# Ten weight chunks of the second layer converted during batch 0's attention, with other buffers for its values and for the first weight quarter

## The chip, the cores and the metric

The kernel runs on one core of a Trainium2 chip. The metric is the device time of one execution in microseconds, as the median of the runs. TensorE (PE) multiplies matrices, VectorE (DVE), ScalarE (ACT) and GpSimd (POOL) work element by element, and SyncE (SP) issues most of the transfers. Each engine, and each queue of transfer issues, works through its instructions in the order in which they stand.

## The reference, cut to what matters

```python
scale = 1.0 / np.sqrt(q.shape[-1])

def sm_attn(qq, kk, vv):
    s = scale * np.matmul(qq, kk.transpose(0, 1, 3, 2))
    s = s - np.max(s, axis=-1, keepdims=True)
    a = np.exp(s)
    a = a / (np.sum(a, axis=-1, keepdims=True) + 1e-09)
    return np.matmul(a, vv)
p_packed = sm_attn(p, k, v)                 # batch 8, heads 8, 32 packed rows, width 64
out = sm_attn(q, p_packed, p_packed)        # 576 rows per batch and head
x = out.transpose(0, 2, 1, 3).reshape(4608, 512)
h = x @ moe_w_in                            # 512 x 2048, float64 in memory
x = (h * np.cos(h)) @ moe_w_out             # 2048 x 512, float64 in memory
h = x @ moe2_w_in
sp = np.where(h > 20.0, h, np.log1p(np.exp(np.minimum(h, 20.0))))
out = (h * np.tanh(sp)) @ moe2_w_out
```

## The kernel before

The weights stand in memory as 64-bit numbers. A chunk of 128 rows and 512 columns of one weight is 512 KB. The helper `conv` loads a chunk and makes 32-bit numbers of it: on ACT an `activation` that reads the high words (L519), on DVE a shift of the low words (L521) and a shift-and-or that joins the two (L525). A chunk of `moe_w_out`, the second layer of the first MLP (`wo1_unit`), is then split into a high and a low part for the matmuls: ACT copies the high part (L534), POOL subtracts to get the low part (L539). Its load goes into one of two buffers named `raw`, and the pieces on the way stand in `tmp` buffers. There are sixteen such chunks. The sixteen chunks of `moe_w_in` (`w_load`, four quarters of four) are converted by the same lines and multiplied by the packed attention values of a batch (L576), and ACT and DVE split the product (L592, L593) into the layer's weights `W1`. So `W1` folds the packed values of a batch into the first layer.

The first MLP runs over 16 tiles of 288 tokens, two tiles per batch, and each tile has 16 steps. A step makes one block of the hidden layer (`l1`, six matmuls into `ps`, L147 to L149), takes it through a chain on ACT, DVE and POOL that makes h cos h (L884, L886, L887, L893, L894, L901, L904), and three steps later multiplies it by one chunk of the second layer (`l2`, twelve matmuls into four `acc` banks). After the sixteenth step the tile is copied out (`evac`, L925 and L927) to `xo`.

Everything that prepares a batch stands in tables by step (`at_pe`, `at_ew`, `at_ld`), which are worked off next to the tiles' steps. Steps below 0 come before the first tile. Batch 0's attention stands at steps from -16 (`PRO`): for each of the two groups of heads g, `k_unit` transposes the keys on TensorE (`e1_pe`, `early_copy`, L201), forms the scores of the packed rows (L288), takes their maximum (L303), their exponential (L311), transposes it (L327, copied by L335 and L336), multiplies it by the values (L353), and leaves the packed result in `pk` (L379). `q_unit(0)` transposes the queries (`e0_pe`), forms the scores against `pk` (L430), and takes them through maximum, subtraction, exponential, sum and scaling (L444, L450, L451, L458, L462, L465, L466, L470) to the first operand of the first layer, `aT` (L475). `behind(mark)` holds an instruction back in the order until a marked one stands.

Within a table entry and between entries a scheduler sets the order on each engine, by priority (`hp`, `tc.high_priority`) and by its own estimate of when an operand is there. The result is one fixed order on each engine.

Before, the values of batch 0 and the first quarter of `moe_w_in` stand in the buffers of the second layer (`wo`, sixteen of them), so that no chunk of the second layer can be written there until they are used. The other three quarters of `moe_w_in` go through the four buffers named `wb`. The chunks of the second layer are placed at steps `ft + WO_OFF`, 0 to 15, their loads two steps earlier.

Of the kernel before, what the change touches and what calls it, by code (L numbers as in the profile page):

```python
# [8 lines left out]
F32 = mybir.dt.float32  # L9
# [26 lines left out]
WO_OFF = 0  # L36
Q0_T = 5
K_OFFS = ((23, 33, 38, 41), (-12, 4, 20, 36), (-4, 4, 19, 39))
# [17 lines left out]
COMB = 240  # L56
HOLD_N = 32
STOP = 0
W0E = (-1, -1, -1, -1)
# [29 lines left out]
def build(tc, q, k, v, p, w1i, w1o, w2i, w2o, out):  # L89
    nc = tc.nc  # L90
    ctx = ExitStack()
    with ctx:
# [121 lines left out]
        def k_unit(b, g, alloc_v):  # L214
# [107 lines left out]
            def s4_pe():  # L322
                e = st["e"]
                t1, t2 = ring(), ring()
                ev = e[:, :512].rearrange("p (t c) -> p c t", c=4)
                for c in range(4):
                    nc.tensor.transpose(t1[:, 128 * c : 128 * c + 128], ev[:, c], ident)  # L327
                nc.tensor.transpose(t2[:, :128], e[:, 448:576], ident)
                st["t"] = (t1, t2)
# [64 lines left out]
        def q_unit(t, pre=None):  # L394
# [25 lines left out]
            def e0_pe():  # L420
                st["kt"] = kt_tile([128, 1152])
                for h in range(4):
                    early_copy(st["kt"], early_trans(st["raw"], h, (0, 0, 1)), h, (0, 0, 1))

# [64 lines left out]

        def conv(src, shape, dst, save, wide=False, st=None, mark=None):  # L490
            st = {} if st is None else st

            def load():
                if wide == "wo":
                    r = wo_tile([128, 512, 2], I32)
                elif wide:
                    w = wab_tile(1, [128, 2048], I32)
                    r = w[:, :1024].rearrange("p (f t) -> p f t", t=2)
                    st["t"], st["m"] = w[:, 1024:1536], w[:, 1536:].bitcast(F32)
                else:  # L500
                    r = tp.tile([128, 512, 2], I32, tag="raw", bufs=2, name=nm("raw"))
                n = shape[-1] if len(shape) == 3 else 512
                if len(shape) == 3:
                    nc.sync.dma_start(r.rearrange("p (a f) t -> p a (f t)", f=n), src.bitcast(I32))
                else:
                    ins = nc.sync.dma_start(r.rearrange("p f t -> p (f t)"), src.bitcast(I32))
                    last_w[0] = getattr(ins, "ins", ins)
                st["r"] = r

            def c1():  # L510
                r = st["r"]
                if wide == "wo":
                    w = wo_tile([128, 1024], I32)
                    st["t"], st["m"] = w[:, :512], w[:, 512:].bitcast(F32)
                elif not wide:
                    st["t"] = tp.tile([128, 512], I32, tag="tmp", bufs=TMP_BUFS, name=nm("cvt"))
                    st["m"] = tmp_tile([128, 512])
                with behind(mark and ("act", *mark)):
# [27 lines left out]
        def w_load(fg, hp, fresh=False):  # L546
            st = {}
            if fresh:
# [4 lines left out]
                    lambda d: w1s.__setitem__((fg, hp), d),  # L553
                    "wo" if fg == 0 else True,
                    st,
# [43 lines left out]
        def wo1_unit(ft):  # L599
# [4 lines left out]

            return conv(w1o[128 * ft : 128 * ft + 128, :], [128, 512], dst, None)

# [171 lines left out]
        for g in range(2):  # L778
            wo = lambda sh: wo_tile(sh, F32)
            wa = lambda sh: wab_tile(0, sh, F32)  # L780
            loads, vl, stages = k_unit(0, g, wo)
            at_ld(PRO - 2, hp(loads, (4 - g) * HP_PRO))
# [17 lines left out]
        for ft in range(16):  # L800
            load, cs = wo1_unit(ft)
            n = ft + WO_OFF
            at_ld(n - 2, load)
            for i, f in enumerate(cs):
# [58 lines left out]

        for n in range(PRO - 4, 0):
            run_bg(bg_pe, n)
            run_ew(n)
# [415 lines left out]
```

## Time and profile before

| | |
|---|---|
| median of 3 runs | 1552.05 us (1551.67 to 1552.79) |
| the profiled execution | 1553.24 us, span 1551.5 us |
| mean granted TensorE clock | 0.984 |
| PE busy (matmuls) | 1472.1 us, 95% of the span |
| DVE, ACT, POOL busy | 1110.1 us (72%), 893.2 us (58%), 639.8 us (41%) |

The profiled execution's time is 1.7 us longer than its span, and 1.2 us above the median. The busy shares are means over stages with different limits; the first 120 us are read apart below. A time of an instruction or a transfer is counted from the start of the span.

### The profile page before, as it was taken

The numbers are of one execution on the slowest core, as the hardware profiler recorded it, in microseconds if no ns is written. First come the engines' busy times: TensorE is split into PE (matmuls) and PEld (weight loads), VectorE is DVE, ScalarE is ACT, GpSimd is POOL, SyncE is SP. The second block draws the span as 40 slices with busy tenths as digits, with TensorE's granted clock in tenths as the row PEclk, the third lists the DMA queues.
The fourth block names the chain that finished last, engine by engine and source line by source line (L and its number), as shares of the span: only waits on it lengthen the run. The fifth ranks groups of instructions, "written<-read, shape, count | busy, mean of one in ns | idle before, by whom it ended". The sixth has DMA issues, their size and how long they took to land.

```text
span 1551.5 us, 29143 instructions
## 1 busy us (share of the span) xinstructions
PE 1472.1 (95%) x9986; PEld 1301.5 (84%) x9986; DVE 1110.1 (72%) x2080; ACT 893.2 (58%) x1850; POOL 639.8 (41%) x634
## 2 busy tenths in 40 slices
PE   6688999999999999999999999999999999999998
PEld 4567778898987989789999887888889898888997
DVE  4895667677676877687775778678678757766756
ACT  3685767667766767667765455334443534454443
POOL 0562323245643645546754666224522512352102
PEclk9899999999999999999999999999999999999999
DMA  8889575445648546633313658668878877867886
GB/s 270 266 227 221 168 179 153 133 108 171 184 128 219 169 136 181 190 93 91 105 50 122 238 212 252 190 203 240 265 217 234 293 217 220 242 212 218 234 261 201
DMA packets 247411, 299.21 MB, mean 193 GB/s; under 512 B 103648, under 2 KB 131040, under 8 KB 247264
## 3 DMA queue, kind: packets, MB, share of 16 engines
q1 hardware_dynamic: 244976, 296.21, 64.2%
q8 instruction: 79, 1.29, 0.4%
q10 hardware_dynamic: 2288, 1.15, 0.3%
q14 instruction: 68, 0.56, 0.1%
HBM read 240.65 MB, written 56.62 MB: 192 GB/s over the span
## 4 chain that ended last, share of the span: by engine, by line
PE 45%; DVE 5%; issue 4%; DMA 3%; POOL 3%; ACT 3%; SPq 1%; DVEq 0%; POOLq 0%; ACTq 0%
PE acc L148 8%; PE acc L149 8%; PE acc L147 8%; PE ps L147 7%; PE ps L148 6%; PE ps L149 6%; POOL ws L643 1%; DMA ws<-wst 1%; DVE wab L979 1%; DVE r L887 1%; DMA raw<-in_moe_w_in_dram 1%; DVE r L886 1%; DMA wst<-ws 1%; POOL gh L1037 0%; ACT wab L978 0%
## 5 line engine op out<-in xcount | busy, mean ns | idle before, releaser
L904 POOL TENSOR_TENSOR gh<-r,gh 128x288 fp32r<-128x288 f32 x256 | 212.4, 838 | 326.1 <-ACT gh L901 227.2
L148 PE MATMUL acc<-gh,wo 128*128 128x288 f32 x1024 | 299.2, 299 | 1.0 <-POOL gh L904 1.0
L149 PE MATMUL acc<-gh,wo 128*128 128x288 f32 x1024 | 295.1, 296 | 0.0
L1037 POOL TENSOR_TENSOR gh<-t,gh 128x512 fp32r<-128x512 f32 (+1 forms) x108 | 144.0, 1337 | 353.9 <-ACT gh L1036 344.4
L147 PE MATMUL acc<-gh,wo 128*128 128x288 f32 x1024 | 276.3, 303 | 1.9 <-ACT gh L901 0.9
L148 PE MATMUL acc<-gh,T 128*128 128x512 f32 (+1 forms) x560 | 207.2, 371 | 2.4 <-DVE gh L1037 1.9
L147 PE MATMUL ps<-wab,ws 128*128 128x512 f32 (+1 forms) x560 | 206.2, 369 | 2.5 <-DMA ws<-wst 1.1
L148 PE MATMUL ps<-wab,ws 128*128 128x512 f32 (+1 forms) x560 | 206.4, 369 | 0.0
L149 PE MATMUL ps<-wab,ws 128*128 128x512 f32 (+1 forms) x560 | 205.3, 369 | 0.0
L149 PE MATMUL acc<-gh,T 128*128 128x512 f32 (+1 forms) x560 | 205.1, 369 | 0.0
L148 PEld LDWEIGHTS acc<-gh,wo 128*128 128x128 f32 x1024 | 193.4, 189 | 8.7 <-issue 5.2
L147 PE MATMUL ps<-aT,wab 128*128 128x288 f32 x512 | 162.4, 318 | 39.2 <-DVE r L894 22.2
L147 PEld LDWEIGHTS acc<-gh,wo 128*128 128x128 f32 x1024 | 183.5, 191 | 15.3 <-issue 5.3
L149 PEld LDWEIGHTS acc<-gh,wo 128*128 128x128 f32 x1024 | 192.7, 189 | 3.1 <-issue 3.0
L893 ACT ACTIVATE r<-r,halfpi 128x288 f32<-128x288 f32 x256 | 135.8, 535 | 89.3 <-DVE r L887 84.8
L1037 DVE TENSOR_TENSOR gh<-wo,gh 128x512 fp32r<-128x512 f32 (+1 forms) x160 | 129.0, 813 | 81.1 <-ACT gh L1036 80.6
L147 PE MATMUL acc<-gh,T 128*128 128x512 f32 (+1 forms) x560 | 181.9, 369 | 1.2 <-DMA T<-tst 1.1
L894 DVE TENSOR_TENSOR r<-r,ps 128x288 f32<-128x288 f32 x256 | 114.3, 449 | 74.0 <-ACT r L893 73.6
L147 PEld LDWEIGHTS ps<-aT,wab 128*128 128x128 f32 x512 | 98.9, 193 | 67.1 <-DVE r L894 30.6
L884 ACT ACTIVATE ki<-ps,quarter 128x288 int32<-128x288 f32 x256 | 125.2, 497 | 51.0 <-PE ps L149 40.8
L148 PE MATMUL ps<-aT,wab 128*128 128x288 f32 x512 | 154.3, 301 | 0.0
L149 PE MATMUL ps<-aT,wab 128*128 128x288 f32 x512 | 153.6, 300 | 0.0
(181 smaller groups left out, 3005.3 us busy)
## 6 DMA issues: line engine op xcount, KB each, us to landing
T<-tst SPq DMA_DIRECT2D x280, 256.0 KB, 3.0
ws<-wst SPq DMA_DIRECT2D x224, 256.0 KB, 3.0
ld<-ws SPq DMA_DIRECT2D x80, 256.0 KB, 3.7
kr<-in_q_dram SPq DMA_DIRECT2D x60, 272.0 KB, 5.8
kr<-in_k_dram SPq DMA_DIRECT2D x56, 272.0 KB, 5.3
tst<-wt SPq DMA_DIRECT2D x56, 256.0 KB, 2.2
wst<-ws SPq DMA_DIRECT2D x56, 256.0 KB, 2.2
x2d<-xo SPq DMA_DIRECT2D x64, 144.0 KB, 1.8
```

Source lines behind the costliest of these rows:

```text
L147: nc.tensor.matmul(ps, l0, r0, start=first, stop=False, skip_group_check=more)
L148: nc.tensor.matmul(ps, l0, r1, start=False, stop=False, skip_group_check=more)
L149: nc.tensor.matmul(ps, l1, r0, start=False, stop=last, skip_group_check=more)
L643: nc.gpsimd.tensor_tensor(w[:, 1], CB[p][K3[k]], w[:, 0], ALU.subtract)
L884: nc.scalar.activation(ki, st["h"], AF.Identity, bias=quarter, scale=1.0 / TWO_PI)
L886: nc.vector.scalar_tensor_tensor(r, ki, -TWO_PI, st["h"], ALU.mult, ALU.add)
L887: (nc.gpsimd if n % C_MOD in C_POOL else nc.vector).tensor_scalar(r, r, 1.570796, -4.712388, ALU.min, ALU.max)
L893: nc.scalar.activation(g, g, AF.Sin, bias=halfpi, scale=1.0)
L894: nc.vector.tensor_tensor(g, g, st["h"], ALU.mult)
L904: nc.gpsimd.tensor_tensor(gh[:, 1], st["g"], gh[:, 0], ALU.subtract)
L979: (nc.gpsimd if k % 2 == 0 else nc.vector).tensor_tensor(x[:, a, 1, :n], src, x[:, a, 0, :n], ALU.subtract)
L1037: eng.tensor_tensor(hl[:, 1, :n], src, hl[:, 0, :n], ALU.subtract)
```

## The change

Ten of the sixteen chunks of the second layer (`WO_EARLY`) are placed at steps -18 to -9 (`WO_AT`), their loads two steps earlier, and the first two loads get a priority ahead of, and level with, batch 0's key loads. For these ten the piece `m` stands in a `gh` buffer. The values of batch 0 go into `ld` buffers, and the first quarter of `moe_w_in` goes through the four `wb` buffers like the others. `q_unit(0)`'s transposes come one step later, and are held behind the transposes of group 1's exponential.

```diff
-Q0_T = 5
+Q0_T = 6
...
+WO_EARLY = 10
+WO_AT = tuple(-18 + ft for ft in range(10))
...
-                nc.tensor.transpose(t2[:, :128], e[:, 448:576], ident)
+                marks[("pe", 1, b, g)] = nc.tensor.transpose(t2[:, :128], e[:, 448:576], ident)
...
-                    early_copy(st["kt"], early_trans(st["raw"], h, (0, 0, 1)), h, (0, 0, 1))
+                    early_copy(st["kt"], early_trans(st["raw"], h, (1, 0, 1)), h, (1, 0, 1))
...
-        def conv(src, shape, dst, save, wide=False, st=None, mark=None):
+        def conv(src, shape, dst, save, wide=False, st=None, mark=None, alt=False):
...
-                if wide == "wo":
-                    r = wo_tile([128, 512, 2], I32)
-                elif wide:
+                if wide:
...
-                if wide == "wo":
-                    w = wo_tile([128, 1024], I32)
-                    st["t"], st["m"] = w[:, :512], w[:, 512:].bitcast(F32)
-                elif not wide:
+                if not wide:
                     st["t"] = tp.tile([128, 512], I32, tag="tmp", bufs=TMP_BUFS, name=nm("cvt"))
-                    st["m"] = tmp_tile([128, 512])
+                    if alt:
+                        st["m"] = ap.tile([128, 2, TT], F32, tag="gh", bufs=GH_BUFS, name=nm("m")).rearrange("p a t -> p (a t)")[:, :512]
+                    else:
+                        st["m"] = tmp_tile([128, 512])
...
-                    "wo" if fg == 0 else True,
+                    True,
...
-            return conv(w1o[128 * ft : 128 * ft + 128, :], [128, 512], dst, None)
+            return conv(w1o[128 * ft : 128 * ft + 128, :], [128, 512], dst, None, alt=ft < WO_EARLY)
...
-            wo = lambda sh: wo_tile(sh, F32)
...
-            loads, vl, stages = k_unit(0, g, wo)
+            loads, vl, stages = k_unit(0, g, ld_tile)
...
-            n = ft + WO_OFF
-            at_ld(n - 2, load)
+            n = WO_AT[ft] if ft < WO_EARLY else ft + WO_OFF
+            at_ld(n - 2, hp(load, (5 - 2 * ft) * HP_PRO) if ft < 2 else load)
...
-        for n in range(PRO - 4, 0):
+        for n in range(PRO - 6, 0):
```

The change moves instructions on every engine. A line of the attention stands two further down in the changed kernel (L311 is L313 there), a line of the first MLP's chain one further up (L884 is L883); the lines of `conv` and of the weight products keep their numbers. Three places are shown.

On ACT, the stretch of batch 0's attention around group 0's exponential. `sm_218` and `sm_259` hold group 0's maximum, `kt` the transposed keys, `raw` a chunk of the second layer as loaded. Before:

```order
L276 COPY pp_135<-ps_133 128x128
L201 COPY kt_137<-et_162 128x288
L276 COPY pp_172<-ps_170 128x128
L201 COPY kt_185<-et_194 128x288
L311 ACTIVATE tmp_234,sm_218<-ps_174,sm_218 128x288
L311 ACTIVATE tmp_234,sm_218<-ps_175,sm_218 128x288
L201 COPY kt_185<-et_210 128x288
```

The same stretch now:

```order
L278 COPY pp_203<-ps_201 128x128
L203 COPY kt_226<-et_235 128x288
L519 ACTIVATE m_162<-raw_119 128x512
L534 CAST wo_205<-m_162 128x512
L203 COPY kt_226<-et_251 128x288
L519 ACTIVATE m_209<-raw_152 128x512
L519 ACTIVATE m_268<-raw_166 128x512
L313 ACTIVATE tmp_285,sm_259<-ps_215,sm_259 128x288
L313 ACTIVATE tmp_285,sm_259<-ps_216,sm_259 128x288
```

The conversions of the third, fourth and fifth chunk of the second layer now stand ahead of group 0's exponential, where none stood.

On DVE, the stretch from the query scores' transposes to the transposes that end batch 0's attention. `sqs` is the softmax sum, `wab_424` and `wab_439` two chunks of `moe_w_in`'s second quarter, and `wab_417` is `W1`. Before:

```order
L444 STREAM_TRANSPOSE tmp_371<-ps_361 128x288
L525 SCALAR_TENSOR_TENSOR wab_424<-wab_424 128x512
L525 SCALAR_TENSOR_TENSOR wab_439<-wab_439 128x512
L444 STREAM_TRANSPOSE tmp_371<-ps_360 128x288
L450 TENSOR_REDUCE mx_377<-tmp_371 128x18
L593 TENSOR_TENSOR wab_417<-ps_410,wab_417 128x512
L462 TENSOR_REDUCE sqs_397<-tmp_371 128x18
L593 TENSOR_TENSOR wab_417<-ps_426,wab_417 128x512
L463 TENSOR_SCALAR sqs_397<-sqs_397 128x18
L465 RECIPROCAL rq_400<-sqs_397 128x18
L470 STREAM_TRANSPOSE tmp_415<-tmp_371 128x576
```

Now, from its beginning, with `pc_928` the packed queries `p` of batch 1 and `wab_491` and `wab_504` two chunks of the second quarter:

```order
L265 STREAM_TRANSPOSE pp_1108<-pc_928 128x128
L446 STREAM_TRANSPOSE tmp_468<-ps_458 128x288
L446 STREAM_TRANSPOSE tmp_468<-ps_457 128x288
L452 TENSOR_REDUCE mx_476<-tmp_468 128x18
L593 TENSOR_TENSOR wab_513<-ps_506,wab_513 128x512
L521 TENSOR_SCALAR wab_491<-wab_491 128x512
L464 TENSOR_REDUCE sqs_493<-tmp_468 128x18
L525 SCALAR_TENSOR_TENSOR wab_491<-wab_491 128x512
L465 TENSOR_SCALAR sqs_493<-sqs_493 128x18
L593 TENSOR_TENSOR wab_513<-ps_522,wab_513 128x512
L521 TENSOR_SCALAR wab_504<-wab_504 128x512
```

A transpose of batch 1 now stands first in this stretch, and the conversions of the second quarter, two of which were ahead of it, stand inside it.

On SP, the loads behind batch 0's queries (`in_q_dram`). Before:

```order
L179 DMA wab_122<-in_q_dram 96x4x192
L506 DMA wo_125<-in_moe_w_in_dram 128x1024
L506 DMA wo_127<-in_moe_w_in_dram 128x1024
L506 DMA wo_129<-in_moe_w_in_dram 128x1024
L506 DMA wo_131<-in_moe_w_in_dram 128x1024
L506 DMA wab_395<-in_moe_w_in_dram 128x1024
L506 DMA wab_408<-in_moe_w_in_dram 128x1024
L506 DMA wab_424<-in_moe_w_in_dram 128x1024
L506 DMA wab_439<-in_moe_w_in_dram 128x1024
L506 DMA raw_448<-in_moe_w_out_dram 128x1024
```

Now, with two chunks of the second layer (`raw_98`, `raw_100`) already issued ahead of the keys:

```order
L181 DMA wab_141<-in_q_dram 96x4x192
L506 DMA raw_119<-in_moe_w_out_dram 128x1024
L506 DMA wab_144<-in_moe_w_in_dram 128x1024
L506 DMA wab_146<-in_moe_w_in_dram 128x1024
L506 DMA wab_148<-in_moe_w_in_dram 128x1024
L506 DMA wab_150<-in_moe_w_in_dram 128x1024
L506 DMA raw_152<-in_moe_w_out_dram 128x1024
L506 DMA raw_166<-in_moe_w_out_dram 128x1024
```

And nine issues further on, where the second quarter of `moe_w_in` is loaded:

```order
L506 DMA raw_375<-in_moe_w_out_dram 128x1024
L506 DMA raw_882<-in_moe_w_out_dram 128x1024
L506 DMA raw_926<-in_moe_w_out_dram 128x1024
L235 DMA pc_928<-in_p_dram 32x4x32 x4
L506 DMA wab_491<-in_moe_w_in_dram 128x1024
L506 DMA wab_504<-in_moe_w_in_dram 128x1024
```

The second quarter's loads have moved from right behind the first quarter's to a place behind twelve chunks of the second layer and batch 1's `p`. From about the 25th step of the first MLP on, every engine's order is the same in both kernels.

## Rows read from the trace of the kernel before

**Rows 1.** Windows: busy time of each engine before and in tile 0.

```profile
core 0: us, PE busy (x) PEld busy (x) DVE busy (x) ACT busy (x) POOL busy (x), PEclk, DMA share, GB/s
0.00:42.60 42.60, 26.23 (x309) 18.25 (x309) 19.39 (x52) 16.61 (x38) 3.01 (x8) 0.93 0.75 245
42.60:117.30 74.70, 59.66 (x436) 48.05 (x436) 67.65 (x129) 58.34 (x113) 44.92 (x38) 0.88 0.89 258
```

**Rows 2.** Timeline, batch 0's attention and tile 0's end: start, duration, idle before.

```profile
16.19 0.50 ACT L311 ACTIVATE tmp<-ps,sm 128x288 f32<-128x288 f32 x1 [2.98 <-DVE sm L305]
...
31.05 0.27 ACT L379 COPY pk<-ps 128x128 f32<-128x128 f32 x1 [1.50 <-PE ps L374]
...
37.98 0.75 DVE L462 TENSOR_REDUCE sqs<-tmp 128x18 f32<-128x576 f32 x1 [1.39 <-ACT tmp L458]
...
42.59 0.61 PE L147 MATMUL ps<-aT,wab 128*128 128x288 f32 x1 [8.78 <-ACT aT L475]
...
117.29 0.69 ACT L925 COPY xo<-acc 128x288 f32<-128x288 f32 x2
```

**Rows 3.** Timeline of SP's issues: chunk loads of 512 KB.

```profile
11.86 0.43 SPq L506 DMA_DIRECT2D wo<-in_moe_w_in_dram  x1
...
16.19 0.33 SPq L506 DMA_DIRECT2D raw<-in_moe_w_out_dram  x1
...
45.08 0.33 SPq L506 DMA_DIRECT2D wab<-in_moe_w_in_dram  x1
```

**Rows 4.** DMA issues, these three alone: size, then us from issue to landing.

```profile
wo<-in_moe_w_in_dram SPq DMA_DIRECT2D x1, 512.0 KB, 7.6
...
raw<-in_moe_w_out_dram SPq DMA_DIRECT2D x1, 512.0 KB, 10.7
...
wab<-in_moe_w_in_dram SPq DMA_DIRECT2D x1, 512.0 KB, 4.0
```

**Rows 5.** Groups of ACT, 5 to 42.6 us (the last: tile 0).

```profile
L519 ACT ACTIVATE wo<-wo 128x512 f32<-128x512 f32 x4 | 2.5, 665 | 0.0
...
L201 ACT COPY kt<-et 128x288 f32<-128x288 f32 x6 | 2.3, 400 | 7.6 <-PE et L190 7.5
L311 ACT ACTIVATE tmp<-ps,sm 128x288 f32<-128x288 f32 x4 | 2.0, 500 | 3.0 <-DVE sm L305 3.0
...
L335 ACT COPY tmp<-ps 128x512 f32<-128x512 f32 x2 | 1.2, 587 | 5.9 <-PE ps L327 5.9
...
L534 ACT CAST wo<-tmp 128x512 fp32r<-128x512 f32 x16 | 9.9, 616 | 4.9 <-DVE tmp L525 4.5
```

**Rows 6.** Groups of DVE by form, 20 to 42.6 us.

```profile
L525 DVE SCALAR_TENSOR_TENSOR wo<-wo 128x512 int32<-128x512 int32 x4 | 2.7, 684 | 0.2 <-ACT wo L519 0.2
...
L521 DVE TENSOR_SCALAR wo<-wo 128x512 int32<-128x512 int32 x4 | 1.4, 421 | 0.0
```

**Rows 7.** Tile p of batches 1 on, 40 to 160 us: its transfers.

```profile
DMA to landing us min/median/max: 3.0/4.7/5.7
```

**Rows 8.** Groups of DVE by form, 42.6 to 117.3 us.

```profile
L525 DVE SCALAR_TENSOR_TENSOR tmp<-tmp,cvt 128x512 int32<-128x512 int32 x16 | 14.6, 918 | 0.4 <-ACT tmp L519 0.3
L521 DVE TENSOR_SCALAR cvt<-raw 128x512 int32<-128x512 int32 x14 | 10.4, 743 | 1.4 <-DMA raw<-in_moe_w_out_dram 1.4
```

**Rows 9.** Line L539, 0 to 140 us: min/median/max ns, first and last start.

```profile
L539 POOL TENSOR_TENSOR wo<-tmp,wo x16: 1274/1511/1749, 44.3 to 110.8; 128x512 fp32r<-128x512 f32 x16
```

**Rows 10.** Windows: tile 0 in four stretches, columns as in group 1.

```profile
42.60:50.30 7.70, 6.92 (x34) 3.86 (x34) 6.10 (x7) 4.32 (x8) 5.87 (x4) 0.71 0.91 272
50.30:60.00 9.70, 3.92 (x16) 3.86 (x16) 9.12 (x20) 8.61 (x18) 3.21 (x4) 0.69 1.02 311
60.00:100.00 40.00, 34.15 (x241) 27.41 (x240) 39.26 (x73) 30.82 (x60) 24.46 (x22) 0.91 0.78 246
100.00:117.30 17.30, 14.67 (x150) 12.92 (x148) 13.17 (x31) 14.59 (x31) 11.38 (x11) 1.00 1.06 251
```

More of the change, by code (lines that the diff above doesn't have):

```diff
@@ L422, in e0_pe @@
                 for h in range(4):
-                    early_copy(st["kt"], early_trans(st["raw"], h, (0, 0, 1)), h, (0, 0, 1))
+                    early_copy(st["kt"], early_trans(st["raw"], h, (1, 0, 1)), h, (0, 0, 1))
             def s2_pe():
```

## Prediction

> **What bounds the kernel now.** I read the busy time by stage first. TensorE is 95% busy over the whole span, so what counts is where it waits, and that is at the start: until 42.6 us it is busy 26.2 us, and in tile 0, from the first matmul of the first layer at 42.59 us to the copying out of the tile at 117.3 us, 59.7 of 74.7 us [rows 1, 2]. In that tile the busiest engine is DVE with 67.65 us; before it, DVE works only 19.4 of 42.6 us [rows 1]. The reader is to see a DVE that is half idle in batch 0's attention and nearly full in tile 0, with the sixteen chunk conversions of the second layer in the full part. The change moves ten of them into the half-idle part. It can gain what DVE's stage shortens by, and lose what batch 0's attention lengthens by, since all of tile 0 starts from that attention's last product. Three lengths decide: the time of the first layer's first matmul (the start, 42.59 now), the length of tile 0 (74.7 now), and their sum (117.3 now). Behind it the orders soon agree and nothing in them gives time back, so I take a shift of the sum as a shift of the end.
>
> **The start: when the loads land.** In the new order on ACT, the conversions of the fourth and fifth chunk stand ahead of group 0's exponential. An engine that waits for a load holds everything behind it, so the exponential can't start before the fifth chunk has landed. Behind keys, `p`, values and queries, the third load of 512 KB was issued at 11.86 us and landed 7.6 later, at 19.5; the ninth was issued at 16.19 and landed 10.7 later, at 26.9 [rows 3, 4]. That is six loads in 7.4 us, one per 1.24 us: the transfers run one behind the other. In the new order the blocks are the same size, only two stand ahead of the keys. So the third chunk is still the third block, and the fifth, which stands behind three chunks, the four loads of the first quarter and one more chunk, is the ninth. It lands at 26.9 us, and after its conversion (0.665 [rows 5]) the exponential starts at 27.6 us, where it was 16.19 [rows 2]: 11.4 later. If the two early blocks fill time in which the transfers now idle, the ninth lands up to 2.5 us (two blocks) sooner.
>
> **The start: ACT's stream.** From that exponential to group 1's `pk` ACT now has, in its order, four exponentials (0.500), nine L519 (0.665), seven L534 (0.616), two L335 (0.587), two L201 (0.400) [rows 5], and two each of L336 and L379, both taken at 0.27 [rows 2]: 2.0 + 6.0 + 4.3 + 1.2 + 0.8 + 1.1 = 15.4 us. The last two L534 follow their own L519 at once and must wait for a shift-and-or on DVE each (0.684 [rows 6]): 1.4 more, if nothing else stands between. So `pk` is there at 27.6 + 16.8 = 44.4 us, where it was 31.3 [rows 2]: 13.1 later. With the sooner landing and no wait it is 40.5.
>
> **The start: from `pk` to the first matmul.** That took 42.59 - 31.32 = 11.3 us [rows 2]. Two things are put in. DVE must first transpose batch 1's `p`, whose transfers stand on SP behind two more chunk loads that need the buffers of the ninth and tenth chunk back. These come free about when `pk` is made; the transfers then land 4.7 us later (3.0 to 5.7 [rows 7]), some 3 us after the scores are there. And the sum of the exponentials (37.98 us now, 6.7 after `pk` [rows 2]) stands behind the first chunk of the second quarter, which can be loaded only when its `wb` buffer has been used, and lands 4.0 us after its issue [rows 3, 4]; that ends at about the same time as the wait for `p`, so the two are not added. I take 2 us for both, between nothing (the waits lie beside each other and beside the chain) and 4 (`p` wholly exposed). The start is then 44.4 + 11.3 + 2.0 = 57.7 us, 15.1 later than now; the bounds are 40.5 + 11.3 = 51.8 and 60.
>
> **Tile 0.** DVE's work there falls by ten shift-and-ors and eight shifts (two were already done before it). At the means of this stage, 0.918 and 0.743 [rows 8], that is 15.1 us; at those before the stage, 0.684 and 0.421, when POOL hardly works [rows 1, 6], it is 10.2. One chunk of the second quarter (0.684 + 0.421 = 1.1) and two transposes come in, some 2.5 together as an estimate from the same rows. So DVE's work becomes 55.0 to 59.9 us; I take the middle, 57.5, as POOL keeps two thirds of its work there.
>
> The longer durations stand where POOL makes the low parts of the same chunks, sixteen times 1.5 us [rows 9]. The Trainium skill's page "SBUF — State Buffer", section "Who interferes with whom", says that a VectorE operation that uses both port pairs and a GpSimd operation lock each other out for a whole instruction. By that page the ten conversions' excess goes with POOL's ten pieces, the work becomes 55.0, and the sum below comes out 2.5 us smaller.
>
> To the work comes DVE's idle time. Now it is 1.6 + 0.6 + 0.7 + 4.1 = 7.0 us over four stretches [rows 10]. The first two, 2.2 us, grow: the third quarter's first load goes out 2.5 us after the first matmul and lands 4.0 later [rows 2, 3, 4], its conversion stands ahead of the first chain, and until then DVE has only a conversion and a split, some 1.8 us, where it had the second layer's chunks to fill the wait. 6.5 - 1.8 is 4.7, so the idle time becomes 4.7 + 0.7 + 4.1 = 9.5 us, and tile 0 takes 67.0 us, 7.7 less than now. Bounds: 59.7, TensorE's own busy time in the stage [rows 1], and 70.
>
> **The sum.** 15.1 later and 7.7 shorter: 7.4 us slower. The profiled execution had 1553.24 us, 1.2 above the median; against that one the sum is 1560.6, against the median of 1552.05 it is 1559.5. The other edits cost nothing that I can see: the `ld` buffers take the values while the `ld` loads of batch 1 are far off, the `gh` buffers are used by the chains only after the tenth chunk, and the query transposes, which leave the way of group 0's exponential, gain nothing as that waits for its load.
>
> **Rivals.** *The loads don't hold the streams, and it is faster.* If the chunks are there when ACT comes to them, five L519 and three L534 (5.2 us) stand ahead of the exponential, most of it in ACT's idle time (16.6 busy of 42.6 [rows 1]); say 2 us late. `pk` then comes at 18.2 + 16.8 = 35.0, the start at 48.3, and tile 0, with a DVE less idle at its beginning, takes 64: 112.3, or 5.0 faster, 1547. It decides from a start before 47.2 with my 67.0, or before 50.2 with 64. For it speaks that ACT has the room; against it that a load in this stretch took 7.6 to 10.7 us to land. *Tile 0 takes up the whole delay.* If TensorE runs through it without waiting, it takes 59.7, and 57.7 + 59.7 = 117.4: no change, 1552. Against it stands that DVE has 57.5 us of work in chains of three engines. *The four `wb` buffers hold the later quarters too.* One more wait of 4.7 us at the fourth quarter moves the tile's end from 57.7 + 67.0 = 124.7 to 129.4 us, 12.1 later than now: 1564. For it: all four quarters share four buffers now. Against it: in tile 0 DVE was nearly full from 60 to 100 us with three quarters of them in the same buffers [rows 10].
>
> That the change doesn't do what it says can be left out: the ten pieces stand ahead of the first matmul in every engine's order.
>
> **How the numbers follow.** My forecast, 1559.5, has 0.48, the faster rival 0.24, the one without change 0.16, the one with the later quarters 0.12. The range runs from the faster rival's 1547 to 1566, where a start of 60 with a tile of 70 would end it (130 against 117.3 is 12.7, so 1565). 0.2%, or 3.1 us, is about what a measurement of this kernel can tell from no change; faster by more than that gets 0.24, within it 0.16, slower 0.60.
>
> **What would show it.** In the changed kernel's profile group 0's exponential would start near 27.6 us with ACT waiting for `raw` ahead of it, `pk` of group 1 near 44, the first matmul of the first layer between 56 and 60, DVE idle for some 5 us after it, and the first tile's copying out near 125. The prediction is wrong if the exponential starts before 22 us, if the first matmul stands before 50, or if tile 0 takes less than 60 us.

## The result and the profile after

The changed kernel takes 1571.68 us (median of 4 runs, 1569.53 to 1573.14), the kernel before beside it 1552.42 (4 runs): a ratio of 1.0120, interval 1.0102 to 1.0138. It is 1.2% or 19.3 us slower, where 7.4 us were forecast. The profiled execution had 1572.67 us, its span 1570.1. In the diff of the change one line is not the kernel's: of `q_unit(0)`'s early work only the transposes moved to a later mark, `early_copy` keeps its mark `(0, 0, 1)`.

First the busy time by stage, as in [rows 1]: columns are the stretch, its length, busy time of PE, PEld, DVE, ACT and POOL with their counts, granted clock, DMA share, GB/s. The cut is the first matmul of the first layer; the last row is a piece of tile 0.

```profile
0.00:60.30 60.30, 29.04 (x308) 19.95 (x308) 33.32 (x70) 27.70 (x56) 17.25 (x18) 0.94 0.80 257
60.30:141.50 81.20, 64.12 (x403) 51.77 (x403) 57.10 (x114) 47.82 (x93) 27.43 (x26) 0.79 0.75 198
...
100.30:110.30 10.00, 5.07 (x22) 1.89 (x22) 9.68 (x18) 7.62 (x12) 5.30 (x5) 0.51 0.42 154
```

The start is at 60.30 us, 17.7 later than in [rows 1]. Tile 0 has 10.6 us less work on DVE and takes 81.2 us, 6.5 more than before. DVE now stands idle for 81.2 - 57.1 = 24.1 us of it (7.0 before), and TensorE's matmuls are busy 64.1 us instead of 59.7 at a granted clock of 0.79 instead of 0.88. In the piece from 100.3 it is 0.51, with DVE full.

The timeline of ACT, as in [rows 2] (start, duration, instruction, and in brackets the idle time ahead of it and who ended it), with lines 2 higher than before up to the attention's end:

```profile
25.69 0.68 ACT L519 ACTIVATE m<-raw 128x512 f32<-128x512 f32 x1 [5.39 <-DMA raw<-in_moe_w_out_dram]
26.97 0.67 ACT L519 ACTIVATE m<-raw 128x512 f32<-128x512 f32 x1 [0.59 <-DMA raw<-in_moe_w_out_dram]
27.53 0.49 ACT L313 ACTIVATE tmp<-ps,sm 128x288 f32<-128x288 f32 x1
...
45.84 0.27 ACT L381 COPY pk<-ps 128x128 f32<-128x128 f32 x1
...
99.58 0.67 ACT L519 ACTIVATE wab<-wab 128x512 f32<-128x512 f32 x1 [3.80 <-DMA wab<-in_moe_w_in_dram]
...
141.47 0.70 ACT L924 COPY xo<-acc 128x288 f32<-128x288 f32 x2
```

Group 0's exponential stands directly behind the fifth chunk, for which ACT waits until 26.97. Of the fourth quarter's last pair of chunks ACT gets the first only at 99.58, 39.3 us behind the start. SP's queue in tile 0 shows when they were issued (start, duration, what is issued, how often):

```profile
62.84 0.81 SPq L506 DMA_DIRECT2D wab<-in_moe_w_in_dram  x2
...
70.43 8.46 SPq L506 DMA_DIRECT2D wab<-in_moe_w_in_dram  x3
...
79.47 0.36 SPq L506 DMA_DIRECT2D wab<-in_moe_w_in_dram  x1
79.88 2.46 SPq L154 DMA_DIRECT2D kr<-in_q_dram  x4
...
83.03 1.02 SPq L154 DMA_DIRECT2D kr<-in_k_dram  x2
...
87.27 1.52 SPq L154 DMA_DIRECT2D kr<-in_k_dram  x2
...
90.80 0.99 SPq L506 DMA_DIRECT2D wab<-in_moe_w_in_dram  x2
```

The last pair is issued 30.5 us behind the start, after eight transfers of queries and keys, and its first chunk takes 8.8 us to its use. DVE's waits in tile 0 (who waited for whom, total us, times, longest), before:

```profile
DVE r L894 <- ACT r L893: 2.3, 3, 1.4
DVE cvt L521 <- DMA raw<-in_moe_w_out_dram: 1.4, 2, 1.2
DVE wab L521 <- DMA wab<-in_moe_w_in_dram: 0.8, 1, 0.8
```

and now:

```profile
DVE wab L521 <- DMA wab<-in_moe_w_in_dram: 6.2, 3, 2.9
DVE wab L593 <- ACT wab L592: 4.4, 2, 2.8
DVE pp L265 <- DMA kr<-in_q_dram: 3.8, 1, 3.8
DVE kt L160 <- DMA kr<-in_k_dram: 3.5, 1, 3.5
DVE r L893 <- ACT r L892: 3.2, 4, 1.2
DVE kt L160 <- DMA kr<-in_q_dram: 1.0, 1, 1.0
```

Waits for landings (`DMA`) make up 14.5 us of them, where they were 2.2 before. So 12.3 of the 17.1 us by which DVE's idle time grew are waits for loads. In stretches as long as those of [rows 10], except for the last:

```profile
60.30:68.00 7.70, 7.53 (x34) 4.55 (x34) 2.12 (x5) 1.81 (x4) 1.59 (x1) 0.61 0.51 175
68.00:77.70 9.70, 6.42 (x31) 6.14 (x35) 8.79 (x20) 8.35 (x16) 2.68 (x4) 0.65 0.49 163
77.70:117.70 40.00, 30.97 (x219) 24.40 (x212) 29.13 (x54) 22.98 (x43) 14.31 (x14) 0.87 0.68 199
117.70:141.50 23.80, 19.20 (x125) 16.68 (x123) 17.06 (x38) 14.68 (x32) 8.85 (x9) 0.78 1.06 218
```

DVE's idle time in them is 5.6, 0.9, 10.9 and 6.7 us; it was 1.6, 0.6, 0.7 and 4.1. And TensorE's timeline at its longest wait inside tile 0, the fourth quarter's products:

```profile
97.42 0.29 PE L151 MATMUL acc<-gh,wo 128*128 128x288 f32 x1
105.23 1.93 PE L576 MATMUL ps<-wab,pk 64*32 64x512 f32 x8 [7.52 <-DVE wab L525]
...
107.74 0.44 PE L151 MATMUL ps<-aT,wab 128*128 128x288 f32 x1
107.98 0.44 PE L149 MATMUL ps<-aT,wab 128*128 128x288 f32 x1
...
111.20 0.29 PE L149 MATMUL ps<-aT,wab 128*128 128x288 f32 x1
111.33 0.29 PE L150 MATMUL ps<-aT,wab 128*128 128x288 f32 x1
```

The loads explain only the first part of this wait: the first chunk of the pair is there at 99.58, and its shift-and-or (L525) starts at 103.34, as DVE's order puts five other instructions behind the chunk's shift, and ends at 105.08. Behind the wait the matmuls start 0.24 us apart, at 111.2 us 0.13: the lower of the clock's two levels (1.2 GHz), then the higher (2.4).

The delay at tile 0's end, 141.47 against 117.29, is 24.2 us. It stays between 22.7 and 24.6 through all sixteen tiles and is 23.9 at the last one's end. The spans differ by 18.6 only. The other 5.3 us are a difference in the second MLP, whose order is the same on every engine: from the sixteenth tile's end to the span's it took 712.5 us in the profile before, 707.2 in this one, and between 707.2 and 711.4 in those of the other kernels below. So it is not shown that the change gives them back.

### The profile page after: what moved, and what is told of

Read it like the earlier page. It is cut to its first block, busy times and chain, and to the rows that moved or that the text cites. A ratio compares the mean times of both kernels' runs of the same rounds, so it can differ in the third digit from the quotient of the medians.

```text
span 1570.1 us, 29139 instructions
## 1 busy us (share of the span) xinstructions
PE 1479.1 (94%) x9986; PEld 1308.4 (83%) x9986; DVE 1109.0 (71%) x2080; ACT 897.6 (57%) x1850; POOL 637.8 (41%) x634
## 4 chain that ended last, share of the span: by engine, by line
PE 51%; DVE 4%; DMA 2%; ACT 2%; issue 1%; POOL 1%; SPq 0%; DVEq 0%; ACTq 0%; POOLq 0%
PE acc L150 9%; PE acc L149 9%; PE acc L151 9%; PE ps L149 8%; PE ps L151 8%; PE ps L150 8%; DMA raw<-in_moe_w_in_dram 1%; DVE r L886 1%; DVE r L885 1%; DMA tst<-wt 0%; POOL wt L678 0%; ACT r L892 0%; DVE r L893 0%; DVE wab L978 0%; PE ps L576 0%
## 5 line engine op out<-in xcount | busy, mean ns | idle before, releaser
L150 PE MATMUL acc<-gh,wo 128*128 128x288 f32 x1024 | 302.8, 300 | 1.4 <-POOL gh L903 1.4
L151 PE MATMUL acc<-gh,wo 128*128 128x288 f32 x1024 | 302.0, 301 | 0.0
L149 PE MATMUL acc<-gh,wo 128*128 128x288 f32 x1024 | 278.3, 302 | 2.4 <-ACT gh L900 2.4
L150 PEld LDWEIGHTS acc<-gh,wo 128*128 128x128 f32 x1024 | 196.4, 192 | 8.8 <-issue 4.9
L151 PEld LDWEIGHTS acc<-gh,wo 128*128 128x128 f32 x1024 | 195.3, 191 | 3.0 <-issue 3.0
L149 PEld LDWEIGHTS acc<-gh,wo 128*128 128x128 f32 x1024 | 184.7, 191 | 15.5 <-ACT gh L900 5.0
L883 ACT ACTIVATE ki<-ps,quarter 128x288 int32<-128x288 f32 x256 | 125.4, 498 | 49.8 <-PE ps L151 39.5
```

The costliest lines, as they stand in the source:

```text
L149: nc.tensor.matmul(ps, l0, r0, start=first, stop=False, skip_group_check=more)
L150: nc.tensor.matmul(ps, l0, r1, start=False, stop=False, skip_group_check=more)
L151: nc.tensor.matmul(ps, l1, r0, start=False, stop=last, skip_group_check=more)
L883: nc.scalar.activation(ki, st["h"], AF.Identity, bias=quarter, scale=1.0 / TWO_PI)
```

## The experiments

The theory after this reading was that two causes add up: the start is late as early conversions wait for their loads in ACT's and DVE's order, and tile 0 is long as all four quarters now pass through four `wb` buffers. The rivals: the conversions' work itself, the lower clock, and DVE's work as the prediction had it. This table holds the two stages of every kernel, from the same windows as above: the start, tile 0's length, in it DVE's work, the time in which TensorE stood still (length less PE busy), and the granted clock. The last column is how much later than before the sixteenth tile ended.

Each row is one profiled execution. Its time lay between 5.5 us above (w_first) and 3.7 below (late4b) the median of its kernel, so differences of two or three us between rows are not shown to come from the edit. Nor is tile 0 always the same work: the scheduler sets a new order for every kernel, and in the kernels without added matmuls between 387 (hold) and 441 (eight_in_wo) were recorded in it. The ratios that are given with the runs are of medians.

| kernel | start | tile 0 | DVE | PE idle | clock | tile 16 |
|---|---|---|---|---|---|---|
| before | 42.6 | 74.7 | 67.7 | 15.0 | 0.88 | 0 |
| changed | 60.3 | 81.2 | 57.1 | 17.1 | 0.79 | 23.9 |
| staging_alone | 45.4 | 77.3 | 70.0 | 18.4 | 0.89 | 3.3 |
| eight_in_wb | 57.6 | 75.8 | 56.0 | 14.6 | 0.83 | 13.4 |
| eight_in_wo | 59.2 | 79.6 | 56.2 | 15.1 | 0.83 | 19.1 |
| no_loads | 52.1 | 78.7 | 55.7 | 16.0 | 0.81 | 15.8 |
| less_dve | 43.5 | 70.4 | 54.3 | 11.2 | 0.89 | -2.2 |
| w_first | 61.4 | 83.8 | 56.2 | 19.9 | 0.84 | 35.2 |
| hold | 58.3 | 73.9 | 56.9 | 16.7 | 0.91 | 20.1 |
| hold_w_first | 56.0 | 82.2 | 60.5 | 19.9 | 0.84 | 19.0 |
| fourth_in_wo8 | 62.5 | 66.8 | 54.6 | 9.1 | 0.91 | 13.7 |
| before_fourth | 43.5 | 77.9 | 70.7 | 15.4 | 0.85 | 2.9 |
| less_dve_fourth | 44.6 | 72.0 | 56.1 | 10.1 | 0.86 | 1.1 |
| late4b | 41.2 | 75.3 | 69.5 | 15.0 | 0.90 | -2.8 |
| filled | 61.5 | 83.7 | 55.1 | 18.5 | 0.90 | 32.3 |
| before_filled | 43.6 | 82.9 | 68.9 | 19.9 | 0.86 | 10.0 |
| late4b_filled | 43.7 | 76.8 | 67.1 | 16.7 | 0.87 | 1.2 |

**Parts of the change: staging alone, eight chunks, the first quarter back in `wo`.**

```
-WO_EARLY = 10
+WO_EARLY = 0    # staging_alone
+WO_EARLY = 8    # eight_in_wb, eight_in_wo
...
-                    True,
+                    "wo" if fg == 0 else True,    # eight_in_wo
```

> No second-layer chunk is converted early; the values stay in ld and the first quarter in wb as in the changed kernel. Theory (two causes: early conversions wait for their loads and hold ACT and DVE, so the start is late; and all four quarters share four wb buffers, so tile 0 is longer): the start falls back to 43 to 47 us, but tile 0 stays at 80 us or more, since the loads of the third and fourth quarter still wait for their buffers; time 1560 to 1567. Rival (what costs is the early conversions' work on ACT and DVE, and the lower clock behind it): both go back, start 43 to 45, tile 0 at 75, time 1551 to 1554.

> Eight early chunks instead of ten, first quarter in wb as in the changed kernel; the control for the next kernel. Theory: the third to fifth chunk still stand ahead of group 0's exponential, so the start is 56 to 60 us, tile 0 79 to 83, time 1567 to 1571. Rival (each early chunk's work costs the same): two chunks of ten less, one fifth of the 19 us back, 1567 to 1568, with the gain at the start.

> Eight early chunks, the first quarter staged in eight of the sixteen wo buffers again. Theory: the start stays late, 55 to 60 us, but the second and third quarter have their wb buffers sooner and tile 0 falls to 66 to 71, so the time is 8 to 14 below that of eight chunks with the quarter in wb: 1554 to 1562. Rival (tile 0 is long through the clock, or through the loads of batch 1's keys and of tile 1's queries): tile 0 stays at 78 or more, time within 3 us of the control.

Measured: staging alone 1.0027 (1.0012 to 1.0042), start 45.4, tile 0 77.3. So the start rises by 2.8 and the tile by 2.6 with no conversion moved; the 80 us that the theory wanted for tile 0 are not there. But this is not the staging by itself. The later query transposes stay in, and so does the priority of the first two loads, which SP issues ahead of its first keys and of the values, and group 0's exponential comes 2.8 us later than in [rows 2]:

```profile
0.74 0.40 SPq L506 DMA_DIRECT2D raw<-in_moe_w_out_dram  x1
...
7.34 0.34 SPq L506 DMA_DIRECT2D raw<-in_moe_w_out_dram  x1
...
19.00 0.50 ACT L313 ACTIVATE tmp<-ps,sm 128x288 f32<-128x288 f32 x1 [3.57 <-DVE sm L307]
```

Eight chunks in `wb`: 1.0058 (1.0036 to 1.0080), a median of 1562.0 us, below what both theory and rival had; in `wo`: 1.0090 (1.0067 to 1.0112). The kernel in which the first quarter has its old buffers back is the slower one, start and tile both, although it was to be 8 to 14 us faster. The part of the theory that blames the first quarter's place is not borne out. Between eight and ten chunks lie 2.7 us of start and 5.4 of tile 0, together a third of the 24.2 us at its end.

**The loads of the early chunks.** The third to tenth chunk read the buffers of the first two again.

```
             def load():
+                if alt and ft > 1:
+                    st["r"] = RAW[ft % 2]
+                    return
```

> Ten early chunks, but the third to tenth are converted from the first two chunks' buffers and never loaded (the second layer's weights are then others): the same work on ACT, DVE and POOL without its loads. Theory (the loads hold the streams): group 0's exponential by 21 us, start 46 to 51, tile 0 as long as with the change, 78 to 83, time 1558 to 1564. Rival (the work itself fills ACT and DVE): exponential at 24 or later, start 56 or later, time 1567 to 1572.

Measured: 1.0081 (1.0061 to 1.0101), 1566.52 us. In ACT's timeline group 0's exponential is at 20.05 and stands behind conversions that wait only for other engines:

```profile
18.26 0.68 ACT L526 ACTIVATE m<-raw 128x512 f32<-128x512 f32 x1 [0.55 <-POOL wo L546]
19.49 0.66 ACT L526 ACTIVATE m<-raw 128x512 f32<-128x512 f32 x1 [0.55 <-POOL wo L546]
20.05 0.49 ACT L313 ACTIVATE tmp<-ps,sm 128x288 f32<-128x288 f32 x1
```

The start falls from 60.3 to 52.1, still 1.1 us above what the theory had, and the time is above its range. Of the start's 17.7 us of delay these eight loads thus make 8.2, the rest of the edits 2.8 (staging_alone; the first two loads are early in both), and what is left, 6.7, goes with the conversions' work. In this kernel the scheduler puts the conversions earlier, so the split is rough. Tile 0 is 2.5 us shorter.

**Conversions behind the exponentials, and the fourth quarter's loads ahead of the next tile's.**

```
-WO_AT = tuple(-18 + ft for ft in range(10))
+WO_AT = (-18, -17) + tuple(-9 + ft for ft in range(8))    # hold, hold_w_first
...
-            at_ld(n - W0_LD if j >= 4 else PRO + W0E[j], load)
+            at_ld(n - W0_LD - 2 * (j > 13) if j >= 4 else PRO + W0E[j], load)    # the w_first ones
...
-                with tc.issue_after(last_w[0]):
+                with tc.issue_after(last_w[0]), tc.issue_after(last_w[1]):
```

> The changed kernel, with the third to tenth chunk loaded and converted nine to sixteen steps before the first layer begins at the latest places, so that both groups' exponentials stand ahead of them. Theory (the loads of these chunks hold ACT and DVE): group 0's exponential at 17 to 20 us, start 47 to 52, tile 0 as long as with the change, time 1559 to 1564. Rival (the chunks' work and their share of the transfers delay the start wherever they stand): start 56 or later, time 1567 to 1572.

> The changed kernel, with the loads of tile 1's queries and batch 1's keys put behind the fourth quarter's loads on SP. Theory B: the fourth quarter's last conversion, 46 us behind the first first-layer matmul with the change, comes at 34 to 40, and tile 0 falls from 81 to 71 to 76, time 1561 to 1566; the start stays at 60. Rival (tile 0 is long because DVE's work is bunched behind the start and the clock falls with every wait): tile 0 stays at 79 to 83, time 1569 to 1573.

> Both edits together. Theory (two causes that add up): start 47 to 52, tile 0 71 to 76, time 1550 to 1557, no better than before or a little worse. Rival: as for the two apart, 1567 or more; if the two causes share one resource, the gain is that of the larger one alone, 1559 to 1563.

Measured: hold 1.0102 (1.0079 to 1.0124), w_first 1.0148 (1.0115 to 1.0182), both 1.0119 (1.0094 to 1.0144). None gains what the theory said. hold's start and time are those of its rival, and so is the time with both edits. In hold the exponential is at 19.09, as expected, and `pk` at 37.34, but the start is at 58.3. TensorE's timeline there:

```profile
37.49 0.63 PE L167 MATMUL ps<-kt,ident 128*128 128x32 f32 x2 [0.73 <-ACT kt L203]
58.34 0.61 PE L149 MATMUL ps<-aT,wab 128*128 128x288 f32 x1 [15.66 <-ACT aT L477]
```

and DVE's, between the scores' sum and its reciprocal (L464, L467) and the transpose behind them (L472):

```profile
47.83 0.74 DVE L464 TENSOR_REDUCE sqs<-tmp 128x18 f32<-128x576 f32 x1
...
50.10 0.68 DVE L525 SCALAR_TENSOR_TENSOR m<-m,cvt 128x512 int32<-128x512 int32 x1
...
51.04 0.25 DVE L467 RECIPROCAL rq<-sqs 128x18 f32<-128x18 f32 x1
51.23 1.57 DVE L525 SCALAR_TENSOR_TENSOR wab<-wab 128x512 int32<-128x512 int32 x1
52.72 1.38 DVE L521 TENSOR_SCALAR wab<-wab 128x512 int32<-128x512 int32 x1
54.20 1.56 DVE L525 SCALAR_TENSOR_TENSOR wab<-wab 128x512 int32<-128x512 int32 x1
...
56.81 0.77 DVE L472 STREAM_TRANSPOSE tmp<-tmp 128x576 f32<-128x576 f32 x1
```

The chain of the scores now waits behind conversions, of early chunks and, longest, of the second quarter, whose loads the change had moved back. At both places that were tried the conversions in batch 0's attention cost the start about as much. In w_first TensorE waits 7.62 us for the transposed queries,

```profile
102.88 0.64 PE L167 MATMUL ps<-kt,ident 128*128 128x32 f32 x2 [7.62 <-DVE kt L160]
```

which stand ahead of the fourth quarter's products in its order. But the edit does not do what it was meant for. The fourth quarter's last two loads are issued 28.7 and 31.1 us behind the start, where it was 30.5, as SP had waited for DVE ahead of them, and the second still stands behind the queries:

```profile
90.16 0.33 SPq L506 DMA_DIRECT2D wab<-in_moe_w_in_dram  x1
90.54 1.89 SPq L154 DMA_DIRECT2D kr<-in_q_dram  x4
92.52 0.55 SPq L506 DMA_DIRECT2D wab<-in_moe_w_in_dram  x1
```

So what SP's order costs tile 0 was not tested.

**DVE's work taken out of tile 0.** In the kernel before, the first ten chunks' two DVE operations are left out; the shift has the same test as the shift-and-or here.

```
             def c2():
+                if part:
+                    return
...
-            return conv(w1o[128 * ft : 128 * ft + 128, :], [128, 512], dst, None)
+            return conv(w1o[128 * ft : 128 * ft + 128, :], [128, 512], dst, None, part=ft < 10)
```

> The kernel before, with the shift and the shift-and-or of the second layer's first ten chunks left out (their weights are then others): nothing is moved, DVE has 20 operations or some 16 us less work in tile 0. Theory A, the one behind the prediction's term for tile 0 (DVE's work sets its length): tile 0 falls from 74.7 to 62 to 68 us, time 1540 to 1546. Theory B (the first layer's fourth quarter sets it: its chunks come late through four buffers and SP's order, however free DVE is): tile 0 stays at 72 to 75, time 1549 to 1553.

Measured: 0.9959 (0.9942 to 0.9976). Tile 0 in windows:

```profile
43.50:113.90 70.40, 59.16 (x395) 49.03 (x395) 54.29 (x111) 56.34 (x111) 41.34 (x37) 0.89 0.90 264
```

13.4 us of DVE's work go and tile 0 becomes 4.3 us shorter: two thirds of what is taken away turns into DVE's idle time, 16.1 us against 7.0. The result lies between the two theories. Taking these operations away for nothing is worth 0.4%. As a ceiling this has two limits. ACT's and POOL's part of the ten chunks and their loads stay in tile 0, where the change takes them out too. And something does move: the scheduler sets another order in tile 0 on every engine.

**The fourth quarter in other buffers.** It is staged in eight `wo` buffers and need not wait until the second and third have been used; in the two made from the kernel before, batch 0's values stand in `ld`.

```
-                    True,
+                    "wo" if fg == 3 else True,    # fourth_in_wo8, with WO_EARLY = 8
+                    "wo" if fg in (0, 3) else True,    # before_fourth, less_dve_fourth
```

> Eight early chunks with the first quarter in wb, as in the run eight_in_wb, but the fourth quarter is staged in eight wo buffers, so it needs not wait until the second and third have passed through the four wb buffers. Theory C (tile 0's length is set by the passage of the quarters through four buffers: in all kernels so far the fourth quarter's last products come 42 to 50 us after the first first-layer matmul, with 54 to 70 us of work on DVE): they come by 35 us, tile 0 falls from 76 to 64 to 70, start unchanged at 57 to 59, time 1552 to 1558. Rival D (DVE, full in the tile's second half, and the clock set it): products sooner, but tile 0 within 3 us of 76, time 1560 to 1565.

> The kernel before with batch 0's values in ld and the fourth quarter in the wo buffers that this frees, beside the first; no chunk is converted early. Theory C: the fourth quarter's products come by 37 us where they came at 47.6, tile 0 falls from 74.7 to DVE's work there, 68 to 71, time 1546 to 1550, faster than before. Rival D (DVE's work sets tile 0 in the kernel before): tile 0 stays at 73 to 76, time 1551 to 1555.

> Both limits of tile 0 eased at once in the kernel before: the fourth quarter in wo buffers, and the shift and shift-and-or of the first ten chunks left out (their weights are then others). Alone, the first gave 70.4 us for tile 0 and the second 77.9, against 74.7. Theory E (two limits of nearly equal length, DVE's work and the quarters' passage through four buffers, so that easing one alone gives little): tile 0 at 61 to 66 us, start at 43 to 45, time 1538 to 1545. Rival (the effects add: 4.3 shorter and 3.2 longer): tile 0 at 73 to 75, time 1550 to 1553.

(In the last one the two figures of the second sentence stand in the wrong order: the fourth quarter in `wo` gave 77.9, less work 70.4.) Measured: 1.0058 (1.0038 to 1.0077), 1.0001 (0.9982 to 1.0020) and 0.9975 (0.9961 to 0.9988). With eight early chunks tile 0 falls from 75.8 to 66.8 at nearly the same work on DVE:

```profile
62.50:129.30 66.80, 57.75 (x392) 46.62 (x393) 54.62 (x108) 48.02 (x93) 31.70 (x29) 0.91 0.67 185
```

The fourth quarter's two products then come 28.5 and 34.4 us behind the start, where eight_in_wb has them at 35.6 and 43.9. But the start is 4.9 later: on the clock of the span the products come 2.2 and 4.6 us earlier and the tile ends 4.1 earlier, so that more than half of the 9.0 us is the later start. After sixteen tiles nothing is left of it (13.7 against 13.4), and the time is the same. So the passage through four buffers makes some 4 us of tile 0's end there, hardly more than the profiles scatter. In the kernel before, the same edit brings the products from 47.6 to 42.9 us only, not to 37, and tile 0 is longer, 77.9, with DVE at 70.7, which neither theory has. With both eased it is 72.0, not 61 to 66, so theory E is not borne out.

**Something for TensorE to do while it waits.** Matmuls that nothing reads, at the first layer's first matmul (40 in the changed kernel, 32 before) and at the fourth quarter's products (28, changed kernel alone).

```
+            if n == 0:
+                fillers(ps, 40, ("w", (0,), 0, 1))
...
+                if bs == (0,) and fg == 3 and g == 0:
+                    fillers(st[0], 28, "mm")
```

> The changed kernel with 68 matmuls of 128x128 that nothing reads, 40 at the first layer's first matmul and 28 at the fourth quarter's products, so that TensorE has something to do in the two waits of 10.0 and 7.5 us. Theory F (each long wait is paid twice: TensorE's matmuls behind it run at half clock for some us): the granted clock in tile 0 rises from 0.79 to 0.85 or more, tile 0 falls by 2 to 5 us, time 1566 to 1570. Rival G (ACT's and DVE's chains set tile 0, so faster matmuls only wait longer): tile 0 within 1.5 us of 81, or longer by what the added matmuls take, time 1570 to 1574.

> The kernel before with 32 such matmuls at the first layer's first matmul, where TensorE waits 8.8 us. Theory F: the clock of the first ten us of tile 0 rises from 0.77 to 0.9 or more, tile 0 falls by 1 to 3 us, time 1549 to 1552. Rival G: tile 0 stays at 74 to 76, time 1551 to 1555.

Measured: 1.0192 (1.0171 to 1.0213) and 1.0018 (1.0004 to 1.0032). In the changed kernel the clock rises from 0.79 to 0.90 as theory F has it, and tile 0 is 2.5 us longer:

```profile
61.50:145.20 83.70, 65.20 (x469) 55.68 (x470) 55.05 (x114) 46.58 (x92) 26.65 (x27) 0.90 0.74 199
```

In both kernels TensorE stands still longer than without them. The scheduler also put some of the added matmuls between the first layer's own, so that their place is part of this. In filled the fourth quarter's last loads were issued 33.0 us behind the start instead of 30.5, and its products came at 51.8 and 55.6 instead of 44.9 and 48.5. In the kernel before the clock of tile 0's first ten us fell, from 0.77 to 0.67, and tile 0 took 82.9 us, so theory F was not tested there. That a higher clock would shorten tile 0 is not borne out, nor is it ruled out.

**A version meant to be faster.** Four chunks, loaded behind everything that the attention needs and converted behind its exponentials; the first and the fourth quarter in `wo`; then with 30 added matmuls.

```
+WO_EARLY = 4
+WO_AT = (-3, -3, -2, -2)
...
+                    "wo" if fg in (0, 3) else True,
```

> A version meant to use this: values in ld, the first and the fourth quarter in wo, and four chunks moved ahead of tile 0, not loaded before the keys and with none of their operations ahead of an exponential of batch 0's attention (two stand before the scores, two at the first layer's first chains). Theory E: the start is 44 to 47, tile 0 66 to 72, the sum 111 to 117, time 1546 to 1552, at best 0.3% faster than before. Rival (each conversion ahead of the first layer costs the start what it saves in tile 0): sum 117 to 121, time 1552 to 1557.

> The version with four chunks converted late and the fourth quarter in wo buffers, with 30 such matmuls at the first layer's first matmul. Theory F: 1 to 3 us below that version, so 1549 to 1552 where the kernel before has 1554 to 1555. Rival G: as that version, 0.1 to 0.2% below before, or lost in the added matmuls.

Measured: 1553.14 us, 0.9985 (0.9971 to 0.9999), and 1549.77, 0.9958 (0.9942 to 0.9973). Both are faster than before, the first hardly beyond the noise, the second by 0.4%, but not as expected: tile 0 has 75.3 and 76.8 us, no less than before. The first has its start 1.4 us earlier. In the second one's profile tile 0 ends 3.2 us later than before, and the sixteenth tile still 1.2 later, while the span is 2.8 shorter (1548.7 against 1551.5). So the profile has the whole gain in the second MLP, 708.6 us against 712.5, where every engine's order is that of before. Whether it comes with the edit or with the execution is open.

## Why the prediction was wrong

**The start was right in its mechanism.** The exponential was to start at 27.6 behind the ninth block and started at 27.53, with ACT waiting for `raw` ahead of it. The ninth block was issued at 18.6 us instead of 16.19 and still landed at 26.9: the blocks land one behind the other, 1.2 to 1.3 us apart. `pk` was there at 46.11 (45.84 and 0.27 for the copy) instead of 44.4, the first matmul at 60.30 instead of 57.7. no_loads shows that these loads hold the stream, and the first rival, that they don't, is gone: without them the exponential is 7.5 us earlier. The start alone was 2.6 us off, 1.7 of it up to `pk`, where ACT waited 4.2 us for DVE and for loads instead of 1.4.

**The step that failed is the length of tile 0:** "the idle time becomes 4.7 + 0.7 + 4.1 = 9.5 us, and tile 0 takes 67.0 us". DVE's work was right, 57.1 us against 57.5. Its idle time is 24.1 us. The forecast took the stage's length as the work of the engine that was full, plus waits that were there before, plus one new one; that holds only while this engine stays the limit. The new wait at the start, put at 4.7 us, was 6.5. The term that failed most is the 0.7 for the middle of the tile: it is 10.9, and the 4.1 at the end became 6.7. In the place of the conversions that left, DVE mostly waits for loads, 14.5 us against 2.2. less_dve points the same way from the other side: in the kernel before, two thirds of the work taken from DVE come back as its idle time, though in another order of all engines. What stands close behind DVE's work is not settled. The passage of the quarters through `wb` is a part (fourth_in_wo8: the tile ends 4.1 us earlier), and DVE's own order another, as the fourth quarter's products started 5.7 us behind the landing of their first chunk. Tile 0 was 7.7 us shorter on paper and 6.5 longer on the chip: 14.2 us. With the start's 2.6 the sum was off by 16.8 us, the time by 11.9.

Of those 6.5 us, 4.5 are matmul time (64.1 against 59.7, at the lower clock, though fewer matmuls are recorded in the tile, 403 against 436) and 2.0 are waits of TensorE. The bound of 59.7, "TensorE's own busy time", was no fixed quantity: it is 57.2 in hold. What the lower clock costs the tile by itself is open, as filled changed more than the clock.

**The third rival** named the right place, the fourth quarter, with a price too small: TensorE's wait there is 7.5 us, not 4.7. That the first quarter's place causes it was not shown; eight_in_wo speaks against it. **The second rival**, tile 0 taking up the delay, is wrong in direction.

**"Nothing gives time back"** holds through the first MLP, 24.2 us at tile 0's end and 23.9 at the sixteenth's. That the spans differ by 18.6 only made the error in the time smaller than the error in the sum, and that is luck as far as is known.

**The longer durations of DVE beside POOL.** The ten shift-and-ors that moved took 0.868 us on average ahead of tile 0, near the 0.918 of [rows 8] and not the 0.684 of [rows 6]; the six that stayed took 1.194. In DVE's groups (count, busy us, mean ns, idle ahead), first the early chunks, then tile 0:

```profile
L525 DVE SCALAR_TENSOR_TENSOR m<-m,cvt 128x512 int32<-128x512 int32 x10 | 8.7, 868 | 1.7 <-ACT m L519 1.2
...
L525 DVE SCALAR_TENSOR_TENSOR tmp<-tmp,cvt 128x512 int32<-128x512 int32 x6 | 7.1, 1194 | 0.1
```

Eight of the ten took 0.69 us. The other two took 1.57, and both started while POOL was making a low part. That is the rule of the Trainium skill's page "SBUF — State Buffer", section "Who interferes with whom", and the trace agrees with it. But the 55.0 us that followed from it for tile 0 were 57.1, since the excess over 0.684 did not leave the tile with the ten: it was 3.7 us for sixteen and is 3.1 for the six that stayed. It decided nothing here.

**Open** is which of the limits sets tile 0 once DVE has less to do: with 54 to 61 us of DVE's work it took between 66.8 and 83.8 us, each edit also changed the scheduler's order, and no run isolates one chain. Open too is what the two loads ahead of the keys cost, as no run takes them back alone, and why late4b_filled is faster.

## What to carry over

An idle engine ahead of a chain is not free room: in engines that work in order, a conversion that waits for its load holds the chain behind it, and here the conversions cost the start 6.7 us more even where eight of the ten had no load of their own. Before moving work out of a full stage, leave it out altogether once, and look whether the order of the rest stayed: here leaving out DVE's part was worth 0.4%, a third of what the move cost. And a stage's length is its fullest engine's work plus waits only until the next limit: work that filled an engine's time between loads leaves a wait for loads behind when it goes.

## What was not expected of the hardware

Behind a wait of 7.5 us matmuls of 128x288 started 0.24 us apart instead of 0.13, with a granted clock of 0.51 from 100.3 to 110.3 us. The first of a pair of 512 KB loads issued behind eight transfers of keys and queries took 8.8 us to its use, where the third quarter's first load took 4.0 to land before [rows 4]. And the second MLP, in the same order on every engine, took between 707.2 and 712.5 us in different kernels' profiles.
